# Attention and gated feed-forward on one core: output stages by a table of places, bias masks on PE for two batches, last keys on GpSimd

## The chip, the cores and the metric

The kernel runs on one core of a Trainium2 chip. The metric is the device time of one execution in microseconds (us). PE is the matrix engine (TensorE), ACT is ScalarE, DVE is VectorE, POOL is GpSimd, SP is SyncE, which only issues transfers here. PSUM is the memory that PE writes its results to; it has 8 banks of 512 fp32 columns, and one matmul writes at most one bank.

## The reference

Eight batches of 576 tokens, 8 heads of 64. Heads 0 to 3 look back over 32 tokens, heads 4 to 7 over 32 tokens at a distance of 4. The result, 4608 tokens of 512 features, goes through a gated feed-forward layer.

```python
batch, n_heads, seq, head_dim = (8, 8, 576, 64)
scores = scale * np.matmul(q, k.transpose(0, 1, 3, 2))
mask_plain = (rel >= 0) & (rel < window)
mask_dil = (rel >= 0) & (rel < window * dilation) & (rel % dilation == 0)
scores = np.where(masks[None, :, :, :], scores, -1000000000.0)
scores = scores - np.max(scores, axis=-1, keepdims=True)
attn = np.exp(scores)
attn = attn / (np.sum(attn, axis=-1, keepdims=True) + 1e-09)
out = np.matmul(attn, v)
...
n_tokens, d_model, d_ff = (4608, 512, 1536)
g = x @ w_gate
gelu = 0.5 * g * (1.0 + erf(g * inv_sqrt2))
val = x @ w_val
return (gelu * val @ w_out).astype(np.float32)
```

## The kernel before

All matmuls are fp16 with fp32 sums. The order of every engine is the order in which the program is written; no scheduler changes it.

**Attention** goes by pairs of heads: n = 0 to 31, four to a batch (n // 4), the first two of a batch plain, the last two dilated. A pair takes three steps. *Scores* (`emit_s`, L310): PE multiplies queries and keys into four PSUM banks (L329 plain, L359 dilated; the last keys of the dilated pairs come from a small copy `kTr`, made by `last_keys` on DVE, L240), and ACT takes the exponential into a tile P (L339 and L340, or L361). *Mask*: either DVE multiplies P by 0 and 1 (L369, `emit_mask`, put into the order later by `mask_next`), or, with `pe_mask`, PE first writes a bias of 0 and -60000 into the four banks by four matmuls with the identity (L322, L345), on which the scores are added, and no mask is needed; before the change the pairs 0 to 3, 6 and 7 do that. *Values* (`emit_pv`, L432): PE multiplies P by the values (the numerator) and by ones (the denominators) into three banks, V to V + 2; then DVE makes the reciprocal by two transposes (`norm_r`: L450, L452, L454) and writes the product to `xT` (`norm_x`: L465 plain, L468 dilated). Until `norm_x` has read them, the three banks aren't free for the next values.

**Feed-forward** goes by nine chunks of 512 tokens (c = 0 to 8). The first layer (`ffn1`, L480) takes 12 blocks `nb`; each writes a gate bank and a value bank, ACT applies Gelu to the gate (L504) and DVE multiplies into `u_all` (L505). Two pairs of banks alternate. `ffn1_two` (L492) does the first two blocks together, a quarter of the features at a time, so that the last quarter of `xT` may come late. The second layer (`ffn2`, L511) takes four blocks of 128 tokens, twelve matmuls `fc` each into one bank, which ACT evicts (`store`, L522), and SP sends out.

**How they are woven.** `mm0` is 0 or 4: the first layer works in the banks mm0 to mm0 + 3, the scores in the other four. In the output stages of chunks 1 to 5 the scores of the next pairs and the values of the last ones (`values_b`) are put between the matmuls of `ffn2`: scores after a block, right behind its eviction, and values inside the next block, at its `fc` 6, 4 and 2; every block but the first writes the bank mm0, the first one V = mm0 + 1. The first scores of a stage stand at the end of the first layer (L661). Where four pairs of values are done in a stage (c = 1 and 2), the fourth comes after the last block, `mm0` changes sides (`late = "x"`), and the next chunk begins with `ffn1_two`; after c = 3, 4 and 5 it stays (`late = "bank"`) and the two pairs of banks change their order.

```python
            ffn2(c, 1, mm0, {6: [pv]})
            store(c, 1, mm0, "act")
            s_next()
            ffn2(c, 2, mm0, {4: [pv]})
            store(c, 2, mm0, "act")
            s_next()
```

**Loads.** SP loads q, k and v of batch c + 2 in chunk c and issues the DMA transposes of the queries and keys (`qTp`, `qTd`); POOL casts to fp16 (L177, L190) and issues the loads of the dilated heads (`qd`, `rd`) and of the weights. In chunk 0 the transposes of batch 1 are done on PE (`t_plain`, `t_dil`, `t_rest`), between first-layer blocks 8 to 11.

Of the kernel before, what the change touches and what calls it, by code (L numbers as in the profile page):

```python
# [38 lines left out]
def kernel(  # L39
# [10 lines left out]
    nc = tc.nc  # L50
# [4 lines left out]
    NHP = H // 2  # L55
    HK = H // 2
# [157 lines left out]
    def load_batch_plain(b):  # L214
# [2 lines left out]
        v_plain(b, sv, nc.sync)  # L217
        return st, sv

    def load_batch_rest(b):  # L220
        st, sv = tiles["plain", b]
        qd, rd = load_qk_dil(b)
        qp = cast_qk_plain(b, st)
        load_v_dil(b)
        v_cast(b, sv)
        new_qt(b)
        qtp_, qtd_, _ = tiles["qT", b]
        dst = qtd_.rearrange("p t h m i -> p (t h m) i")
        nc.sync.dma_start_transpose(out=dst[:, :, 0:P], in_=qd.rearrange("p t h r d -> p (t h r d)"))
        nc.sync.dma_start_transpose(out=dst[:, :, P:NCL], in_=rd.rearrange("p t h r d -> p (t h r d)"))  # L230
        dst = qtp_.rearrange("p t h c -> p (t h) c")
        for kb in range(5):
            n = min(P, S - kb * P)
            nc.sync.dma_start_transpose(
                out=dst[:, :, kb * P : kb * P + n], in_=qp[0:n, kb].rearrange("p t h d -> p (t h d)")
            )

    def last_keys(b, h0, h1):
        _, qtd_, ktr = tiles["qT", b]
        nc.vector.tensor_copy(ktr[:, h0:h1], qtd_[:, 1, h0:h1, :, NCL - 64 : NCL])  # L240


    def is_plain(n):
# [66 lines left out]
    def emit_s(n, b0, pe_mask=False):  # L310

        b, hp = n // NHP, n % 2
        qtp_, qtd_, ktr = tiles["qT", b]
        st = not pe_mask
        mm = nc.tensor.matmul
        if n % NHP == 0 and n >= NHP:
            last_keys(b, 0, HK)
        if is_plain(n):
            if pe_mask:
                for i in range(4):  # L320
                    src = bias_p[:, 0:PB] if i % 2 == 0 else bias_p[:, PB:PH]
                    mm(ps[:, b0 + i, 0 : src.shape[1]], ident, src, start=True, stop=False, skip_group_check=True)  # L322
            for j in (0, 1, 2, 3, 4):
                for hl in range(2):
                    kt = qtp_[64 * hl : 64 * hl + 64, 1, hp, :]
                    qt = qtp_[64 * hl : 64 * hl + 64, 0, hp, :]
                    bank, c0 = b0 + 2 * hl + j // 3, (0, PW, 2 * PW, 0, P)[j]
                    k0, q0, w = (j * P, j * P, P if j == 3 else PW) if j < 4 else (S - P, S - PT, PT)
                    mm(  # L329
                        ps[:, bank, c0 : c0 + w],  # L330
                        kt[:, k0 : k0 + P],
                        qt[:, q0 : q0 + w],
                        start=st,
                        stop=True,
                        skip_group_check=True,
                    )
            pt = prb.tile([P, 2, PH], F16, tag="P", name=f"P{n}")
            sb = ps[:, b0 : b0 + 4, :].rearrange("p (h t) c -> p t h c", t=2)
            nc.scalar.activation(pt[:, :, 0:PB], sb[:, 0, :, 0:PB], AF.Exp, bias=0.0, scale=scale)  # L339
            nc.scalar.activation(pt[:, :, PB:PH], sb[:, 1, :, 0 : P + PT], AF.Exp, bias=0.0, scale=scale)  # L340
            reps, mask, w = 2, mask_p, PH
        else:
            if pe_mask:
                for i in range(4):
                    mm(ps[:, b0 + i, 0:DW], ident, bias_d, start=True, stop=False, skip_group_check=True)  # L345
            for hl in range(2):
                h = 2 * hp + hl
                for m in range(3):
                    for s in range(2):
                        half = slice(64 * s, 64 * s + 64)  # L350
                        bank = ps[:, b0 + 2 * s + hl, 0:DW]
                        if m < 2:
                            o = bank[:, m * NCL : m * NCL + P]
                            lhs, rhs = qtd_[half, 1, h, m, 0:P], qtd_[half, 0, h, m, 0:P]
                        else:
                            o = bank.rearrange("p (m i) -> p m i", m=2)[:, :, P:NCL]
                            lhs = ktr[half, h].rearrange("p m i -> p (m i)")
                            rhs = qtd_[half, 0, h, :, P:NCL]
                        mm(o, lhs, rhs, start=st, stop=True, skip_group_check=True)  # L359
            pt = prb.tile([P, 4, DW], F16, tag="P", name=f"P{n}")  # L360
            nc.scalar.activation(pt, ps[:, b0 : b0 + 4, 0:DW], AF.Exp, bias=0.0, scale=scale)  # L361
            reps, mask, w = 4, mask_d, DW
        tiles["P", n] = pt
        if pe_mask:
            return None

        def emit_mask():
            mb = bass.AP(tensor=mask.tensor, offset=mask.offset, ap=[mask.ap[0], [0, reps], [1, w]])
            nc.vector.tensor_tensor(pt, pt, mb, ALU.mult)  # L369

        return emit_mask
# [252 lines left out]
    scores = {0: range(4, 8), 1: range(8, 12), 2: range(12, 17), 3: range(17, 22), 4: range(22, 27), 5: range(27, 32)}  # L624
    values_b = {1: range(8, 12), 2: range(12, 16), 3: range(17, 20), 4: range(22, 24), 5: range(27, 28)}
    values_a = {3: {4: 16}, 4: {3: 20, 6: 21}, 5: {2: 24, 4: 25, 6: 26}, 6: {1: 28, 3: 29, 5: 30, 7: 31}}
    late = None
    for c in range(NCH):
        if 1 <= c and c + 2 < B:
# [2 lines left out]
        pv_at = values_a.get(c, {})  # L632
        s_list = list(scores.get(c, ()))
        pairs = (mm0, mm0 + 2)
        SB = 4 - mm0

        masks = []
        pend = None
        for nb in range(NNB):
            if nb == 0 and c < 2:  # L640
                ffn1_two(c, (4, 6) if c == 0 else (6, 0))
            elif nb == 0 and late == "x":
                ffn1_two(c, pairs)
            elif nb > 1 or c > 2 and late != "x":
                ffn1(c, nb, pairs[(nb + (c < 2 or late == "bank")) % 2])
            if pend is not None:
                norm_x(pend, SB)
                pend = None
            if nb in pv_at:
                pend = pv_at[nb]  # L650
                emit_pv(pend, SB, wide=True)
                norm_r(pend, SB, wide=True)
            if c == 0 and nb in (8, 9):
                t_plain(1, q61, nb - 8, 4 + 2 * (nb - 8), ("act", "dve"))
            if c == 0 and nb in (10, 11):
                rr = rd1.rearrange("p t h r d -> p t (h r d)")
                hp = nb - 10
                t_dil(1, hp, qd1, 4096 + 512 * hp, 5120 + 512 * hp, ("dve", "dve"))
                t_rest(1, hp, (rr[:, 0], rr[:, 1]), 6144 + P * hp)
            if nb == NNB - 1 and c > 0 and s_list:  # L660
                masks.append(emit_s(s_list.pop(0), SB))  # L661

        def s_next():
            if s_list:
                n = s_list.pop(0)
                masks.append(emit_s(n, SB, pe_mask=n in (6, 7)))

        def mask_next():
            mask = masks.pop(0) if masks else None
            if mask is not None:  # L670
                mask()

        def norm(n, b0):
            norm_r(n, b0)
            norm_x(n, b0)
# [8 lines left out]
        if c == 0:  # L684
# [9 lines left out]
            store(c, 3, 1, "act")  # L694
            num(6, 2)
            num(7, 4)
        elif c in values_b:
            todo = list(values_b[c])

            def pv(last=False):  # L700
                if todo and (len(todo) > 1 or last or len(values_b[c]) < 4):
                    n = todo.pop(0)
                    emit_pv(n, V)
                    if not last:
                        mask_next()
                    norm(n, V)

            mask_next()
            ffn2(c, 0, V)
            store(c, 0, V, "act")  # L710
            s_next()
            ffn2(c, 1, mm0, {6: [pv]})
            store(c, 1, mm0, "act")
            s_next()
            ffn2(c, 2, mm0, {4: [pv]})
            store(c, 2, mm0, "act")
            s_next()
            ffn2(c, 3, mm0, {2: [pv]})
            store(c, 3, mm0, "act")
            s_next()  # L720

            late = "bank"
            if todo:
                pv(last=True)
                mm0 = 4 - mm0
                late = "x"
            while masks:
                mask_next()
        else:
            late = None  # L730
            for tb in range(4):
                ffn2(c, tb, mm0 + tb)
                store(c, tb, mm0 + tb, "act" if tb < 3 else "dve")
# [1 line left out]
_INS = ['q', 'k', 'v', 'moe_w_gate', 'moe_w_val', 'moe_w_out']  # L735
_OUTS = [((4608, 512), 'float32')]
# [25 lines left out]
```

## Time and profile before

| | |
|---|---|
| median of 7 runs | 365.35 us (364.33 to 366.11) |
| profiled execution | 364.81 us; its span, first to last instruction, 362.9 us |
| granted clock of PE | 0.995 of full speed |
| busy: PE, DVE, ACT, POOL | 340.8, 193.7, 144.3, 75.9 us |
| chain that ended last | PE 72%, DMA 12%, DVE 9%, ACT 3%, POOL 2% |

The span begins with loads (until about 52 us, when the last output weights have landed), then chunk follows chunk. An output stage of chunks 1 to 5 begins at 88.24, 129.16, 169.07, 208.54 and 247.30 us. Of the profile's lists, a group is read as: line, engine, operation, tile written <- tiles read, shapes, count; the bracket of a timeline's line holds the idle time before it and what ended it. Matmul ends are modelled, so the lengths below go from start to start.

### The profile page before, as it was taken

How to read it: one execution, taken by the hardware profiler on the slowest of the kernel's cores; microseconds unless marked ns; L12 is line 12 of the kernel's file. 1: busy time of each engine (PE TensorE's matmuls, PEld its weight loads, DVE VectorE, ACT ScalarE, POOL GpSimd, SP SyncE). 2: the span in 40 equal slices, each digit the busy share in tenths (PEclk: the TensorE clock that was granted, in tenths of full speed). 3: DMA queues.
4: the chain of work that ended last, by engine and by line, in shares of the span. 5: the costliest groups of instructions: out<-in, count | busy, mean ns of one | idle time of the engine just before them, and what ended most of it. 6: DMA issues, size and time to landing. Idle time of an engine off the chain costs nothing.

```text
span 362.9 us, 6010 instructions
## 1 busy us (share of the span) xinstructions
PE 340.8 (94%) x2368; PEld 162.1 (45%) x2368; DVE 193.7 (53%) x292; ACT 144.3 (40%) x212; POOL 75.9 (21%) x104
## 2 busy tenths in 40 slices
PE   6889899999889999899989999999999999999995
PEld 2544444444444444444444444444444444444442
DVE  1584456643785348763766656783479413303320
ACT  2633345335333353525453355325542223312321
POOL 2580524530630620052004400150000000000000
PEclk9989999999999999999999999999999999999999
DMA  8999999999999991798149932795100030011002
GB/s 203 233 188 226 190 169 183 201 145 252 177 154 273 175 163 60 185 172 115 60 129 186 156 63 96 167 150 80 60 29 2 0 116 2 1 58 60 0 29 87
DMA packets 107291, 45.30 MB, mean 125 GB/s; under 512 B 83040, under 2 KB 102496, under 8 KB 107264
## 3 DMA queue, kind: packets, MB, share of 16 engines
q1 hardware_dynamic: 84272, 31.21, 39.8%
q0 software_dynamic: 21456, 12.01, 27.0%
q10 hardware_dynamic: 1536, 1.70, 2.1%
q8 instruction: 18, 0.29, 0.3%
q14 instruction: 9, 0.07, 0.1%
HBM read 40.13 MB, written 9.44 MB: 137 GB/s over the span
## 4 chain that ended last, share of the span: by engine, by line
PE 72%; DMA 12%; DVE 9%; ACT 3%; POOL 2%; issue 1%; ACTq 0%; SPq 0%; DVEq 0%; POOLq 0%
PE ps L480 42%; PE ps L511 22%; PE ps L432 4%; DMA xT<-in_k_dram 3%; DMA st<-in_k_dram 3%; DMA wv<-in_moe_w_val_dram 3%; DMA wo<-in_moe_w_out_dram 2%; DVE xT L468 2%; DVE rb L454 2%; DVE dt L450 2%; PE ps L492 2%; DVE P L369 1%; ACT osb L522 1%; DMA sv<-in_v_dram 1%; DVE u_all L505 1%; ACT P L361 1%
## 5 line engine op out<-in xcount | busy, mean ns | idle before, releaser
L505 DVE SCALAR_TENSOR_TENSOR u_all<-g,ps 128x512 f16<-128x512 f16 x108 | 73.6, 687 | 86.3 <-PE ps L480 76.8
L504 ACT ACTIVATE g<-ps 128x512 f16<-128x512 f32 x108 | 63.6, 597 | 123.8 <-PE ps L480 114.3
L511 PE MATMUL ps<-wo,u_all 128*128 128x512 f16 x432 | 101.0, 379 | 4.7 <-ACT osb L522 3.0
L480 PE MATMUL ps<-xT,wg 128*128 128x512 f16 x400 | 102.8, 379 | 1.3 <-DVE xT L468 1.1
L480 PE MATMUL ps<-xT,wv 128*128 128x512 f16 x400 | 102.6, 379 | 0.0
L511 PEld LDWEIGHTS <-u_all 128*128 128x128 f16 x432 | 39.8, 98 | 48.8 <-issue 4.9
L480 PEld LDWEIGHTS <-wv 128*128 128x128 f16 x400 | 39.2, 98 | 47.2
L480 PEld LDWEIGHTS <-wg 128*128 128x128 f16 x400 | 37.9, 98 | 46.4 <-issue 2.8
L522 ACT ACTIVATE osb<-ps 128x512 f32<-128x512 f32 x33 | 19.7, 597 | 66.2 <-PE ps L511 66.1
L190 POOL CAST qp<-st 128x2048 f16<-128x2048 f32 x6 | 11.4, 1896 | 109.9 <-DMA sv<-in_v_dram 74.9
L450 DVE STREAM_TRANSPOSE dt<-ps 128x576 f32<-128x576 f32 x32 | 24.9, 778 | 5.1 <-PE ps L432 4.8
L454 DVE STREAM_TRANSPOSE rb<-rc 128x576 f32<-128x576 f32 x32 | 24.9, 778 | 1.1
L369 DVE TENSOR_TENSOR P<-P,mask_p 128x1344 f16<-128x1344 f16 x14 | 13.3, 954 | 14.6 <-ACT P L340 14.6
L361 ACT ACTIVATE P<-ps 128x1152 f16<-128x1152 f32 x16 | 18.0, 1127 | 7.3 <-PE ps L359 7.3
L369 DVE TENSOR_TENSOR P<-P,mask_d 128x1152 f16<-128x1152 f16 x12 | 9.8, 820 | 15.7 <-ACT P L361 15.7
L468 DVE TENSOR_TENSOR xT<-ps,rb 128x576 f16<-128x576 f32 x16 | 17.9, 1127 | 0.4
L524 DVE TENSOR_SCALAR osb<-ps 128x512 f32<-128x512 f32 x3 | 2.1, 692 | 28.8 <-PE ps L511 28.8
L339 ACT ACTIVATE P<-ps 128x960 f16<-128x960 f32 x16 | 15.5, 968 | 1.5 <-PE ps L329 1.4
L432 PE MATMUL ps<-P,ones 128*64 128x96 f16 (+5 forms) x216 | 14.7, 248 | 1.1 <-ACT P L361 0.7
L492 PE MATMUL ps<-xT,wg 128*128 128x512 f16 x32 | 12.2, 380 | 0.9 <-DVE xT L468 0.9
L492 PE MATMUL ps<-xT,wv 128*128 128x512 f16 x32 | 12.1, 379 | 0.5 <-DMA wv<-in_moe_w_val_dram 0.5
L465 DVE TENSOR_TENSOR xT<-ps,rb 128x576 f16<-128x576 f32 x16 | 11.9, 750 | 0.8 <-PE ps L432 0.5
(74 smaller groups left out, 232.2 us busy)
## 6 DMA issues: line engine op xcount, KB each, us to landing
out_dram<-osb SPq DMA_DIRECT2D x36, 256.0 KB, 2.0
sv<-in_v_dram SPq DMA_DIRECT2D x40, 128.0 KB, 3.5
st<-in_q_dram SPq DMA_DIRECT2D x24, 128.0 KB, 3.1
st<-in_k_dram SPq DMA_DIRECT2D x24, 128.0 KB, 3.3
qd<-in_q_dram POOLq DMA_DIRECT2D x7, 256.0 KB, 5.4
qd<-in_k_dram POOLq DMA_DIRECT2D x7, 256.0 KB, 7.1
vd<-in_v_dram POOLq DMA_DIRECT2D x7, 256.0 KB, 7.3
wg<-in_moe_w_gate_dram POOLq DMA_DIRECT2D x3, 512.0 KB, 7.3
```

The lines of the kernel that those rows point to most:

```text
L361: nc.scalar.activation(pt, ps[:, b0 : b0 + 4, 0:DW], AF.Exp, bias=0.0, scale=scale)
L369: nc.vector.tensor_tensor(pt, pt, mb, ALU.mult)
L432: nc.tensor.matmul(o, lhs, rhs, start=st, stop=True, skip_group_check=True)
L450: nc.vector.transpose(dst, den)
L454: nc.vector.transpose(rb.rearrange("p (b c) -> p b c", c=32), bass.AP(tensor=rc.tensor, offset=rc.offset, ap=[rc.ap[0], [1, 18], [0, 32]]),)
L468: nc.vector.tensor_tensor(dst.rearrange("p (i m s) -> p i m s", m=2, s=2), num, rb.rearrange("p (s m i) -> p i m s", s=2, m=2), ALU.mult,)
L480: nc.tensor.matmul(ps[:, b0 + gi, :], w[:, kc, ns], xT[kc][:, tok], start=(kc == 0), stop=(kc == NKC - 1))
L492: nc.tensor.matmul(ps[:, pairs[nb] + gi, :], w[:, kc, ns], xT[kc][:, tok], start=(kc == 0), stop=(kc == NKC - 1),)
L504: nc.scalar.activation(g, ps[:, b0, :], AF.Gelu)
L505: nc.vector.scalar_tensor_tensor(u_all[:, nb, :], g, USCALE, ps[:, b0 + 1, :], ALU.mult, ALU.mult)
L511: nc.tensor.matmul(ps[:, bank, :], u_all[:, fc, tb * P : (tb + 1) * P], wo_t[fc // 4][:, fc % 4, :], start=(fc == 0), stop=(fc == NNB - 1),)
L522: nc.scalar.activation(osb, ps[:, bank, :], AF.Copy, bias=0.0, scale=1.0 / USCALE)
```

## The change

The output stages of chunks 1 to 5 are now laid out by a table. An entry such as `2.6v` means: in block 2, before matmul 6, the values of the next pair; `1.12s` means: after block 1 and its eviction, the scores of the next pair. Within a stage scores and values alternate so that some stand at block boundaries too.

Beside that: pairs 8 to 15 (batches 2 and 3) get their mask as a bias on PE. `last_keys` of batches 2 to 7 is a copy by GpSimd at the end of the batch's load. The first output block of a stage writes a bank of the first-layer pair that was used last but one (`first`). The bank side `mm0` now changes after chunk 3 too (more than two pairs of values), and chunk 4 begins with `ffn1_two`. In chunk 0 the PE transposes of batch 1 change order: dilated pair 0 after block 8, plain ones after 9 and 10, dilated pair 1 after 11.

```diff
+    def last_keys(b, h0, h1, eng=nc.vector):
+        _, qtd_, ktr = tiles["qT", b]
+        eng.tensor_copy(ktr[:, h0:h1], qtd_[:, 1, h0:h1, :, NCL - 64 : NCL])
...
+        last_keys(b, 0, HK, nc.gpsimd)
...
-        if n % NHP == 0 and n >= NHP:
+        if n == NHP:
             last_keys(b, 0, HK)
...
+    biased = (6, 7, 8, 9, 10, 11, 12, 13, 14, 15)
+    four = "1.5s 1.9v 1.12s 2.6v 2.12s 3.3v 3.12s 3.12v"
+    three = "1.4s 1.12v 2.3s 2.12v 3.2s 3.12s 3.12v"
+    two = "1.4s 1.12v 2.3s 2.12v 3.2s 3.12s"
+    one = "1.4s 1.12v 2.3s 2.12s 3.6s"
+    places = {1: four, 2: four, 3: three, 4: two, 5: one}
...
-            if c == 0 and nb in (8, 9):
-                t_plain(1, q61, nb - 8, 4 + 2 * (nb - 8), ("act", "dve"))
-            if c == 0 and nb in (10, 11):
+            if c == 0 and nb in (9, 10):
+                t_plain(1, q61, nb - 9, 4 + 2 * (nb - 9), ("act", "dve"))
+            if c == 0 and nb in (8, 11):
...
-                masks.append(emit_s(n, SB, pe_mask=n in (6, 7)))
+                masks.append(emit_s(n, SB, pe_mask=n in biased))
...
+            first = pairs[(NNB - 2 + swap) % 2] + (pairs[(NNB - 2 + swap) % 2] == mm0)
+
+            def pv(last):
+                n = todo.pop(0)
+                emit_pv(n, V)
+                if not last:
+                    mask_next()
+                norm(n, V)
...
+                bank = mm0 + tb if not lone else first if tb == 0 else mm0
+                ffn2(c, tb, bank, hooks)
+                store(c, tb, bank, "dve" if c > 5 and tb == 3 else "act")
+                for fc, kind in at:
+                    if fc == NNB:
+                        do(kind, True)
+            if lone:
+                late = "bank"
+                if len(values_b[c]) > 2:
+                    mm0 = 4 - mm0
+                    late = "x"
```

## The prediction

> **What bounds the kernel now.** I read the page first, then the windows of the five output stages that the change rewrites, then PE's waits, then PE's timeline inside them.
>
> ```profile
> span 362.9 us, 6010 instructions
> ...
> PE 340.8 (94%) x2368; PEld 162.1 (45%) x2368; DVE 193.7 (53%) x292; ACT 144.3 (40%) x212; POOL 75.9 (21%) x104
> ```
>
> PE is the bound, the others are half idle. So only two things count: work added to PE, and holes in PE.
>
> ```profile
> 88.24:107.62 19.38, 15.85 (x173) 8.27 (x173) 14.03 (x18) 9.34 (x12) 9.48 (x11) 1.00 1.24 171
> 129.16:146.72 17.56, 16.06 (x184) 8.29 (x183) 12.28 (x19) 9.54 (x14) 1.03 (x2) 1.00 0.55 112
> 169.07:186.20 17.13, 15.41 (x163) 7.76 (x163) 12.50 (x18) 9.09 (x13) 0.00 (x0) 1.00 0.26 64
> 208.54:224.19 15.65, 14.55 (x146) 7.21 (x145) 9.96 (x14) 7.94 (x11) 0.00 (x0) 1.00 0.28 70
> 247.30:262.09 14.79, 13.71 (x125) 6.63 (x125) 7.00 (x10) 7.93 (x11) 0.00 (x0) 1.00 0.17 59
> ```
>
> Each row is one output stage, c = 1 to 5, from the end of its first-layer matmuls to the first matmul of the next chunk; the second figure is its length, the third PE's busy time. PE idles 3.53, 1.50, 1.72, 1.10 and 1.08 us: 8.9 us in all. The clock is 1.00, so nothing is to be had there.
>
> ```profile
> PE ps L511 <- ACT osb L522: 3.0, 10, 0.3
> PE ps L432 <- DVE xT L468: 2.1, 3, 1.1
> PE ps L511 <- DVE u_all L505: 1.4, 3, 0.5
> PE ps L432 <- DVE xT L465: 1.3, 1, 1.3
> ```
>
> Ten waits for the evicted bank, three for the last `u_all`, the rest for the bank of the values before.
>
> ```profile
> 89.25 2.75 PE L511 MATMUL ps<-wo,u_all 128*128 128x512 f16 x12 [0.45 <-DVE u_all L505]
> 91.93 0.47 PE L329 MATMUL ps<-qTp 64*128 64x160 f16 x10
> 92.33 1.47 PE L511 MATMUL ps<-wo,u_all 128*128 128x512 f16 x6
> ...
> 96.60 1.02 PE L511 MATMUL ps<-wo,u_all 128*128 128x512 f16 x4 [0.31 <-ACT osb L522]
> 98.88 0.45 PE L432 MATMUL ps<-P,vp 128*64 128x160 f16 x8 [1.25 <-DVE xT L465]
> ...
> 106.96 0.30 PE L432 MATMUL ps<-P,vd 128*64 128x128 f16 x4 [1.08 <-DVE xT L468]
> ```
>
> This is stage 1: the first output block waits for `u_all`; scores of 0.40 stand between two blocks, shorter than the eviction of the bank, so PE waits 0.31 more; and the values of a head pair wait until DVE has turned the values before into `xT` and so emptied their banks, 1.25 and 1.08.
>
> ```profile
> 212.34 0.60 ACT L522 ACTIVATE osb<-ps 128x512 f32<-128x512 f32 x1 [1.42 <-PE ps L511]
> 212.83 1.12 ACT L361 ACTIVATE P<-ps 128x1152 f16<-128x1152 f32 x1
> ...
> 220.98 0.96 ACT L339 ACTIVATE P<-ps 128x960 f16<-128x960 f32 x1
> 221.83 0.50 ACT L340 ACTIVATE P<-ps 128x384 f16<-128x384 f32 x1
> ```
>
> On ACT an exponential starts 0.49 after an eviction's start, and a plain one ends 1.35 after its own start (220.98 to 221.83 + 0.50).
>
> **Prices, from starts in PE's timeline (us).** An L511 matmul 0.216 (twelve 2.59). Plain scores 0.50 (91.93 to 92.33 is 0.40, and 0.10 to switch in); dilated 0.47. Values: plain 0.81 (0.09 in, 174.03 to 174.75), dilated 0.75 (214.00 to 214.66). A bank is writable again 0.85 after its block's last slot (slot end 95.75, eviction 95.95 to 96.55, matmul 96.60). Values to values, when nothing else is in DVE's way: plain 3.56 (174.03 to xT's end at 177.54, and 0.05), dilated 3.89 (214.00 to 217.89).
>
> **Bias on PE, n = 8 to 15.** Four matmuls each. Dilated: four L345 take 0.49 (59.99 to 60.48 on the chain of waits, with the switch that scores pay anyway). Plain: no row in a warm stage; below, 0.49 for fewer columns (1152 against 1344); above, 0.67, the two prologue groups of L322 (10.51 to 11.18, 11.58 to 12.25) with 0.10 of switch in it. I take 0.57, L345 scaled by columns and equally 0.67 less the switch. Sum 4 x (0.57 + 0.49) = 4.24 on PE. By the Trainium skill (TensorE: Matmul & The Clock Gate, Back-to-back issue gap) sustained 512-column matmuls come every 131 ns, which would make the bias an estimated 2.6 and the time 361.7 instead of the forecast below. In this trace they come every 216 ns, over twelve at 89.25 as anywhere, and that decides. DVE loses eight L369 masks (0.86 and 0.76; two were stretched to 2.24 and 1.50).
>
> **The stages, walked from 0 at the end of the first layer.** A comma is the next step of PE; "free" is when a wait lets go.
>
> *c = 1.* Biased scores 8 to 1.07, block 0 to 3.66: it goes to bank 2, freed a block earlier, so the 0.45 for `u_all` goes; the bias that now stands ahead covers the rest. Five matmuls to 4.74, biased scores 9 to 5.81, four to 6.67, values 8 (start 6.76) to 7.49, three to 8.14. Bank free 8.99; biased scores 10 last to 9.10: no wait. Six to 10.40, values 9 start 10.49 (free 6.76 + 3.56 = 10.32) to 11.22, six to 12.52, scores 11 to 13.48 (free 13.37), three to 14.13, values 10 start 14.22 (free 14.05) to 14.88, nine to 16.82. Values 11 wait for values 10: 14.22 + 3.89 = 18.11, to 18.77. Before 19.38: **-0.61**. The 1.2 wait at the end stays.
>
> *c = 2.* The same walk to 16.80 (banks 5 and 4 are free, no `u_all` wait before either), then unbiased scores 16 to 17.30; values 15 at 18.09, to 18.75. Before 17.56: **+1.19**. It had no `u_all` wait and small eviction waits, so 2.12 of bias buys 0.93.
>
> *c = 3.* Scores 17 to 0.50, sixteen to 3.95, scores 18 to 4.42, eight to 6.15, values 17 to 6.96, free 7.00, three to 7.65, scores 19 to 8.12, nine to 10.06, values 18 to 10.81, free 10.91, two to 11.34, scores 20 to 11.84, ten to 14.00, scores 21 to 14.50, values 19 (start 14.59) to 15.25. The banks now swap here, so the next chunk begins in the banks of scores 21: eviction from 14.19, their exponentials from 14.68 to 16.05, and the second matmul goes at 16.10 instead of 15.47, 0.63 late. The last quarter waits for values 19 (18.48), to 19.34; 0.20 for `g` as after c = 1 and 2 now; masks 20 and 21 (2 x 0.86) stand before `u_all` on DVE: 0.49. The third pair ends at 21.75; before at 17.13 + 24 x 0.216 = 22.31: **-0.56**.
>
> *c = 4.* Scores 22 to 0.47 and no `u_all` wait (the pairs' order changes with the swap), sixteen to 3.92, scores to 4.39, eight to 6.12, values 22 to 6.87, free 6.97, three to 7.62, scores to 8.12, nine to 10.06, values 23 (free 10.10, start 10.15) to 10.81, free 10.91, two, scores to 11.84, ten, scores 26 to 14.47. Before 15.65: **-1.18**.
>
> *c = 5.* Scores 27 to 0.47, sixteen to 3.92, scores to 4.42, eight, values 27 to 6.90, free 7.00, three, scores to 8.15, nine to 10.09, scores 30 to 10.56, free 10.94, six, scores 31 to 12.71, six to 14.01. Before 14.79: **-0.78**.
>
> **What costs nothing.** Last keys on GpSimd: no row for this copy; 0.49 (128x256, L178) to 1.05 (128x1024, L177), I take 0.72 (128x512, L250). It waits for both transposes, and behind it stand the next batch's `qd` loads: issued at 102.04 before, at most 104.48 + 0.72 = 105.2 now, landing near 113.4 instead of 110.24. SP transposes them from 119.09: 5 us of cover; keys are wanted later still. Without cover it would be the 3.2. DVE's 0.29 each was no wait of PE. Chunk 0: dilated transposes now come first and wait for `rd` (landed 42.68) instead of the 1.08 for `qp`; PE is some 0.25 later, but it waits for `wo` (landed 52.54) in either case, arriving at 52.18 before. Below nothing this can't go: that landing hangs on loads and POOL alone.
>
> **Sum.** -0.61 + 1.19 - 0.56 - 1.18 - 0.78 = -1.94. Span 362.9 to 361.0; the profiled execution took 364.81, 1.9 of it outside the span, so 362.87. The median of the runs is 365.35, and I state the forecast against it: 363.4.
>
> **Rivals.** *Slower: the hooks come too early.* In c = 1 and 2 values 9, 10, 13 and 14 start 0.17 after their bank is free. If DVE needs e longer than the rows, PE waits at two hooks, all matmuls of the output block queued behind, and again at the last values: 2 (e - 0.17) + e = 3e - 0.34 a stage. From e = 0.44 the gain is gone; at 0.8 it is 6 x 0.8 - 0.68 = 4.12 lost, 367.5. For it: the trace has 93.73 to 98.88, 5.15 instead of 3.56. Against: that was the 2.24 mask, beside a POOL cast, and it is gone. The Trainium skill (SBUF — State Buffer, Who interferes with whom) lets GpSimd's reads block only a VectorE operation with two SBUF inputs or a two-port mode; by it L465 stays clear and e is nothing. Chance 0.14.
>
> *No change.* The hand-over after c = 3 costs more than walked, because `u_all` is behind the two masks: if both are paid in full, 1.72 instead of 0.49, and the plain bias costs 0.67 (4 x 0.10 more), 1.94 - 1.23 - 0.40 = 0.31 is left: 365.0. For it: the chunk now starts in the banks emptied last; against: `u_all` waits for `g` anyhow. Chance 0.12.
>
> *More.* That hand-over is free (0.63 + 0.20 + 0.49 less), as it is before the change, where the next chunk starts in other banks: 362.1. Against: ACT's order is written, and store 3 and scores 21 stand right ahead. Chance 0.12. That the built program doesn't do it is excluded: its order has the bias matmuls before n = 8 to 15 and the new places.
>
> **Numbers.** My sum 0.62. Range 361.8 to 365.2: down to the free hand-over with 0.3 of spread, up to e = 0.43. The measurement tells about 0.2%, 0.73 us. Faster 0.62 + 0.12 = 0.74, same 0.12, slower 0.14.
>
> **What would show it.** Right: the five stages become 18.8, 18.8, 15.7 (to the first matmul; 0.9 of it is given back in the next 3.5 us), 14.5 and 14.0 long; "PE L511 <- DVE u_all" vanishes; "PE L511 <- ACT osb" falls from 3.0 to about 0.8; eight masks fewer on DVE. Wrong: waits of the values' matmuls for `xT` above 0.2 at 2.6v and 3.3v, or new waits for `qTd` or `kTr`.

## The result and the profile after

The changed kernel takes 364.19 us (median of 25 runs, 362.49 to 366.01) beside 365.57 for the kernel before (64 runs): a ratio of 0.9961, 95% interval 0.9951 to 0.9972, so 1.0 to 1.8 us faster. The forecast was 1.95 us faster, 363.4 us. The profiled execution took 364.58 us at a granted clock of 0.984 (before: 364.81 at 0.995). In the changed kernel the lines stand a little lower than before: L511 is now L512, L432 is L433, the masks' L369 is L370, L522 is L523.

The head of the page after:

```profile
span 362.5 us, 6061 instructions
...
PE 347.2 (96%) x2400; PEld 165.8 (46%) x2400; DVE 185.7 (51%) x278; ACT 146.1 (40%) x212; POOL 78.3 (22%) x110
```

PE is busy for 6.4 us more and the span is 0.4 shorter: the change bought out holes and paid for it in matmuls. Not all of the 6.4 is added work. Some 3.8 lie in stages 1 and 2, where the bias was added (17.66 and 18.07 below, 15.85 and 16.06 before); 2.3 lie in the first 53 us, where about the same matmuls ran at a lower granted clock in this execution (0.90 up to 53.78 us, before 0.97 up to 52.58). The windows of the five stages, as before from the last first-layer matmul's slot to the first matmul of the next chunk, and as fourth row the first layer that follows stage 3 (start:end, length, PE busy):

```profile
90.08:108.84 18.76, 17.66 (x189) 9.15 (x187) 8.80 (x13) 9.69 (x12) 7.23 (x10) 1.00 1.11 160
130.40:149.19 18.79, 18.07 (x200) 9.58 (x198) 8.82 (x13) 9.73 (x13) 3.09 (x5) 1.00 0.66 118
171.52:187.27 15.75, 15.23 (x163) 7.70 (x163) 8.97 (x13) 9.53 (x13) 0.00 (x0) 1.00 0.33 78
187.27:210.07 22.80, 22.75 (x128) 10.19 (x127) 16.33 (x25) 8.70 (x15) 8.86 (x12) 1.00 0.95 168
210.07:224.57 14.50, 14.45 (x145) 7.03 (x145) 9.37 (x13) 8.28 (x11) 0.00 (x0) 1.00 0.38 85
247.66:261.70 14.04, 13.70 (x126) 6.57 (x126) 6.83 (x10) 9.04 (x11) 0.00 (x0) 1.00 0.16 59
```

Walked were 18.77, 18.75, 15.7, 14.47 and 14.01. PE now idles 1.10, 0.72, 0.52, 0.05 and 0.34 in them, 2.7 us against 8.9. PE's waits from 90 us to the end of stage 5 (releaser: us in total, times, longest):

```profile
PE ps L433 <- DVE xT L469: 1.8, 2, 1.1
PE ps L493 <- DVE xT L469: 0.9, 2, 0.5
PE ps L493 <- ACT P L340: 0.5, 1, 0.5
PE ps L512 <- ACT osb L523: 0.3, 1, 0.3
```

The wait for the last `u_all` is gone, that for the evicted bank is down from 3.0 in ten to 0.3 in one. That one stands in stage 5; what else is left stands at the ends of stages 1 and 2, in the first layers behind them, and at the hand-over after stage 3. PE's timeline of stage 1 shows the beginning and the end:

```profile
90.08 0.73 PE L323 MATMUL ps<-bias_p,ident 128*128 128x480 f16 x4
...
91.14 3.84 PE L512 MATMUL ps<-wo,u_all 128*128 128x512 f16 x17
...
108.18 0.30 PE L433 MATMUL ps<-P,vd 128*64 128x128 f16 x4 [1.10 <-DVE xT L469]
```

Seventeen output matmuls run without a hole (from 91.14) where twelve had waited 0.45 before; the last values still wait 1.10 for DVE.

### The profile page after: what moved, and what is told of

It reads as the page before. It is cut to its first block, busy times and chain, and to the rows that moved or that the text cites. A ratio compares the mean times of both kernels' runs of the same rounds, so it can differ in the third digit from the quotient of the medians.

```text
span 362.5 us, 6061 instructions
## 1 busy us (share of the span) xinstructions
PE 347.2 (96%) x2400; PEld 165.8 (46%) x2400; DVE 185.7 (51%) x278; ACT 146.1 (40%) x212; POOL 78.3 (22%) x110
## 4 chain that ended last, share of the span: by engine, by line
PE 78%; DMA 13%; DVE 4%; POOL 2%; ACT 1%; issue 0%; SPq 0%; ACTq 0%; POOLq 0%; DVEq 0%
PE ps L481 41%; PE ps L512 25%; PE ps L433 5%; DMA xT<-in_k_dram 3%; DMA st<-in_k_dram 3%; DMA wv<-in_moe_w_val_dram 3%; PE ps L493 3%; DMA wo<-in_moe_w_out_dram 2%; DVE xT L469 1%; PE ps L360 1%; DMA sv<-in_v_dram 1%; PE ps L330 1%; DVE dt L451 1%; DVE rb L455 1%; DMA out_dram<-osb 1%; PE ps L346 1%
## 5 line engine op out<-in xcount | busy, mean ns | idle before, releaser
L512 PE MATMUL ps<-wo,u_all 128*128 128x512 f16 x432 | 101.1, 380 | 0.6 <-ACT osb L523 0.3
L512 PEld LDWEIGHTS <-u_all 128*128 128x128 f16 x432 | 39.2, 98 | 44.9 <-issue 1.0
L481 PEld LDWEIGHTS <-wv 128*128 128x128 f16 x392 | 38.3, 98 | 46.4 <-issue 0.2
L523 ACT ACTIVATE osb<-ps 128x512 f32<-128x512 f32 x33 | 19.7, 598 | 48.4 <-PE ps L512 48.4
L433 PE MATMUL ps<-P,ones 128*64 128x96 f16 (+5 forms) x216 | 15.1, 254 | 2.0 <-ACT P L362 1.0
L370 DVE TENSOR_TENSOR P<-P,mask_p 128x1344 f16<-128x1344 f16 x10 | 9.1, 914 | 6.8 <-ACT P L341 6.8
L370 DVE TENSOR_TENSOR P<-P,mask_d 128x1152 f16<-128x1152 f16 x8 | 6.1, 757 | 11.1 <-ACT P L362 11.1
```

What stands on the lines that cost most here:

```text
L433: nc.tensor.matmul(o, lhs, rhs, start=st, stop=True, skip_group_check=True)
L481: nc.tensor.matmul(ps[:, b0 + gi, :], w[:, kc, ns], xT[kc][:, tok], start=(kc == 0), stop=(kc == NKC - 1))
L512: nc.tensor.matmul(ps[:, bank, :], u_all[:, fc, tb * P : (tb + 1) * P], wo_t[fc // 4][:, fc % 4, :], start=(fc == 0), stop=(fc == NNB - 1),)
L523: nc.scalar.activation(osb, ps[:, bank, :], AF.Copy, bias=0.0, scale=1.0 / USCALE)
```

## Experiments

Stage lengths below are by the same windows: from the end of the first layer's last slot.

**Was stage 1 of before really 19.38 long?** The kernel before twice more, nothing edited.

> The kernel before, unchanged: a second look at its start and its stage 1. Theory A (after the trace of the old stages behind the new chunk 0 showed stage 1 at 18.2 us and chunk 1 starting at 89.9): the first trace of before was lucky in its start (88.3) and unlucky in stage 1 (19.3), because masks and GpSimd's casts met; here chunk 1's output stage starts at 89 to 90.5 us and stage 1 is 18.0 to 19.4 us, the later the start, the shorter or longer as the masks meet the casts; stages 2 to 5 stay 17.5, 17.0, 15.6, 14.7. Rival: stage 1 is 19.3 and the start 88.3 again, and the new order of chunk 0 makes the difference.

> The kernel before, unchanged, a third look: as for the second. Theory A: the start of stage 1 and its length differ from look to look by 0.5 us or more, stages 2 to 5 by less than 0.05. Rival: all are as in the first trace.

Measured: 365.02 and 364.61 us. The output stage of chunk 1 began at 89.26 and 89.39 us. Stages 2 to 5 agree with the first trace within 0.02 us. Stage 1 was 18.55 and 18.05 long, against 19.38 in the trace that the prediction used; a fourth trace with the same stage 1 (the old table with the new chunk 0, below) has 18.31. The rows that differ, all engines, first the trace of the prediction:

```profile
93.55 1.90 POOL L190 CAST qp<-st 128x2048 f16<-128x2048 f32 x1 [13.28 <-DMA sv<-in_v_dram]
...
93.91 2.24 DVE L369 TENSOR_TENSOR P<-P,mask_p 128x1344 f16<-128x1344 f16 x1 [2.19 <-ACT P L340]
```

and the second of the new ones:

```profile
95.07 0.86 DVE L369 TENSOR_TENSOR P<-P,mask_p 128x1344 f16<-128x1344 f16 x1 [2.18 <-ACT P L340]
...
95.68 2.00 POOL L190 CAST qp<-st 128x2048 f16<-128x2048 f32 x1 [14.56 <-DMA st<-in_k_dram]
```

The mask of pair 9 takes 2.24 when GpSimd's cast began 0.36 ahead of it, and 0.86 when it began 0.61 ahead of the cast. The other two traces lie between; the first of the new ones, then the one with the new chunk 0:

```profile
93.75 1.89 POOL L190 CAST qp<-st 128x2048 f16<-128x2048 f32 x1 [14.16 <-DMA st<-in_k_dram]
94.93 1.42 DVE L369 TENSOR_TENSOR P<-P,mask_p 128x1344 f16<-128x1344 f16 x1 [2.19 <-ACT P L340]
```
```profile
94.07 1.89 POOL L190 CAST qp<-st 128x2048 f16<-128x2048 f32 x1 [13.68 <-DMA sv<-in_v_dram]
95.49 1.18 DVE L369 TENSOR_TENSOR P<-P,mask_p 128x1344 f16<-128x1344 f16 x1 [2.18 <-ACT P L340]
```

In the three traces where the cast came first, the mask ends 0.70 to 0.71 after the cast, and the stage goes with the mask: 19.38, 18.55, 18.31 and 18.05 long for masks of 2.24, 1.42, 1.18 and 0.86. When that cast comes depends on when its data land (the bracket), so stage 1 differs from run to run. The Trainium skill says that a VectorE operation with two SBUF inputs contends with a GpSimd instruction that reads SBUF, and that the order of issue decides which of them blocks (SBUF — State Buffer, Who interferes with whom); these rows agree. Over the four traces stage 1 of before is 18.57 long on average; after the change, which has no mask there, six traces give 18.76 to 18.78. So the stage did not become 0.6 shorter, but some 0.2 longer than those four were on average.

**Does the bias pay?** The changed kernel with the bias taken off pairs 8 to 15, and with it for batch 2 alone; then the kernel before with the bias alone.

```diff
-    biased = (6, 7, 8, 9, 10, 11, 12, 13, 14, 15)
+    biased = (6, 7)                      # e2_no_bias
+    biased = (6, 7, 8, 9, 10, 11)        # e3_bias_batch2
```
```diff
-                masks.append(emit_s(s_list.pop(0), SB))
+                n = s_list.pop(0)
+                masks.append(emit_s(n, SB, pe_mask=n in range(6, 16)))
...
-                masks.append(emit_s(n, SB, pe_mask=n in (6, 7)))
+                masks.append(emit_s(n, SB, pe_mask=n in range(6, 16)))   # e6_before_bias
```

> The changed kernel with the masks of pairs 8 to 15 on DVE again. Theory A (walk with the prediction's prices): the 4.24 us of bias go from PE, the masks come into DVE's chain. Stage 2, where GpSimd casts nothing, falls from 18.8 to 17.9 us. In stage 1 masks 9 and 10 fall into GpSimd's casts and are stretched: 17.9 without stretching, 19.4 with two stretches of 0.7 to 1.4 us. In all 0.9 us faster to 0.6 slower than the changed kernel. Rival: the bias pays in both stages, because DVE's chain is what values wait for; then both stages grow, to 19.5 or more, and the time rises by 1.4 us or more.

> The changed kernel with the bias for batch 2 alone (pairs 8 to 11); batch 3 has masks on DVE. Theory A: stage 1 stays 18.8 us, stage 2 falls to 17.9, the time falls by 0.9 us against the changed kernel, to 0.9937 of the kernel before. Rival (the bias pays in both): stage 2 grows to 19.5, the time rises by 0.7 us.

> The kernel before with the bias masks of pairs 8 to 15 on PE and nothing else. Theory A (the prediction's prices walked in the old order): stage 1 falls from 19.3 to 18.5 us, since the bias fills the waits for the evicted bank and for u_all, stage 2 grows from 17.5 to 18.5; in all 0.1 us, the same time as before within 0.1%; the table of places is then worth nothing in these two stages. Rival: the bias needs the new places to fill the waits; then both stages grow by 1 to 2 us and the time is 2 to 3 us longer.

Measured: 363.34 us without the new biases (7 runs; ratio to before 0.9951, 0.9934 to 0.9969), 363.52 with batch 2's alone (6; 0.9949, 0.993 to 0.9968), and 366.48 for the kernel before with all of them (12; 1.0026, 1.001 to 1.0043). Stages 1 and 2 of the kernel without:

```profile
89.68:108.33 18.65, 15.79 (x174) 8.20 (x173) 12.82 (x17) 9.47 (x12) 8.99 (x11) 1.00 1.14 149
129.88:147.92 18.04, 16.12 (x183) 8.41 (x183) 11.78 (x17) 9.64 (x14) 3.09 (x5) 1.00 0.83 131
```

PE has 1.9 us less work in each stage (third figure, 15.79 against 17.66), but the stages are only 0.11 and 0.75 shorter: both end when DVE has done the norms of three pairs, one after the other, and the bias mostly fills time that PE would spend waiting. In stage 1 of this trace the masks of pairs 9 and 10 were stretched as well, to 1.23 and 1.51 from 0.86 and 0.76; so without such stretching the bias may be dearer there. In the old order the bias makes stage 2 18.56 long instead of 17.56, and leaves stage 1 at 18.57. Where it was put, then, the bias costs about 0.9 us in the new order by the stage lengths, and 0.9 in the old one by the times (366.48 against 365.59 for the kernel before beside it). In the new order the times alone don't show it: 363.34 is 0.85 below 364.19, but as ratios to the kernel before it is 0.9951 against 0.9961, with intervals that overlap.

**What else was in the change.** The old order of chunk 0's transposes in the changed kernel (e1) and the new order in the kernel before (e5); the last keys on DVE again (e7); the first output block in V, the bank of the values, as before (e8, one run).

```diff
-            if c == 0 and nb in (9, 10):
-                t_plain(1, q61, nb - 9, 4 + 2 * (nb - 9), ("act", "dve"))
-            if c == 0 and nb in (8, 11):
+            if c == 0 and nb in (8, 9):
+                t_plain(1, q61, nb - 8, 4 + 2 * (nb - 8), ("act", "dve"))
+            if c == 0 and nb in (10, 11):          # e1_old_chunk0; e5 is the reverse, in the kernel before
...
-        last_keys(b, 0, HK, nc.gpsimd)
...
-        if n == NHP:
+        if n % NHP == 0 and n >= NHP:              # e7_dve_keys
...
-                bank = mm0 + tb if not lone else first if tb == 0 else mm0
+                bank = mm0 + tb if not lone else V if tb == 0 else mm0      # e8_block0_in_V
```

> The changed kernel with the order of batch 1's PE transposes in chunk 0 put back (plain pairs after blocks 8 and 9, dilated ones after 10 and 11). Theory A, the prediction's: chunk 0 ends on the landing of the last output weights in either order, so the time is that of the changed kernel, 0.9961 of the kernel before, within 0.1%, and the stages of chunks 1 to 5 stay 18.8, 18.8, 15.8, 14.5, 14.0 us. Theory B: the missing part of the forecast gain (1.94 forecast, some 1.4 measured) was lost in chunk 0, where PE now waits for the dilated rows; then the time falls by 0.5 us or more, to 0.9947 or less.

> The kernel before with the changed order of batch 1's transposes in chunk 0 and nothing else; its trace is also a second look at the old output stages behind another start. Theory A (the new order is hidden by the wait for the last output weights): 1.000 of the kernel before within 0.1%. Theory B (the new order costs what is missing of the forecast): 0.4 to 0.9 us slower, 1.001 to 1.0025. On the stages, theory A: they are fixed and stay 19.3, 17.5, 17.0, 15.6, 14.7 us, so that the whole of the missing part lies ahead of chunk 1. Rival: stage 1 of the one trace of before was unlucky, with two masks stretched by GpSimd's casts; then it is shorter here, 18.0 to 18.8 us, and the gain of the change was never 2.2.

> The changed kernel with the last keys copied by DVE again, at the first scores of each batch. Theory A: DVE's 0.29 us copies wait for nobody, and the five stages keep 18.8, 18.8, 15.6, 14.4 and 13.9 us within 0.1. Outside the span the changed kernel spends 2.08 us (median of 25) against 1.9 to 1.95 before and in the kernels that are before with one edit; if GpSimd's copies are the reason, it is 1.95 here and the time falls by 0.15, else it stays 2.08. Rival: the copies sit in DVE's chains of stages 1 and 2 and lengthen each by 0.3 us.

> The changed kernel with the first output block of a stage in bank V again. Theory A: in stage 1 the bias covers the wait for u_all, in 3 and 4 the two banks are the same, so only stage 5 grows, by 0.5 us (13.9 to 14.4). Rival: the freed bank matters in every stage with the other order of pairs, 0.4 to 0.5 us in stage 1 too.

*Chunk 0*: 363.77 us with the old order in the changed kernel (12 runs; 0.9965, 0.9952 to 0.9977), the same as the change itself; 365.25 with the new order in the kernel before (12; 0.9989, 0.9971 to 1.0006). Neither swap moves the time by more than the intervals, about 0.6 us each way. The begin of stage 1 scatters by more than that: from 88.2 to 89.8 us in five traces with the old order (mean 89.3) and from 89.3 to 90.6 in nine with the new one (mean 89.9). So a cost of some tenths stays open. The reason that was given for a cost of nothing, that PE waits for the last output weights in either order, holds in the traces of before and after, but in only five of the fourteen in all; in these two PE comes when the weights are already there.

*Keys*: 364.16 us on DVE again (12 runs; 0.9957, 0.9939 to 0.9974): no difference. The two groups, of the changed kernel and of this one:

```profile
L222 POOL COPY kTr<-qTd x6: 614/615/617, 78.8 to 245.4; 128x512 f16<-128x512 f16 x6
```
```profile
L222 DVE COPY kTr<-qTd x8: 280/290/434, 18.3 to 251.3; 128x512 f16<-128x512 f16 x8
```

GpSimd takes 0.615 us for what DVE does in 0.29; the prediction had taken 0.72. Nothing on PE waits for either. One small thing does go with it. The time that a run takes beyond its span is 1.94 us at the median for the kernel before, 2.08 for the changed one, 2.07 to 2.15 for every other variant of several runs with keys on GpSimd, and 1.96 for this one: some 0.13 us that no row of the span shows.

*First block*: 365.28 us in one run; its stages 1 to 4 are as in the changed kernel, stage 5 is 0.53 longer. PE's timeline there:

```profile
248.76 2.10 PE L512 MATMUL ps<-wo,u_all 128*128 128x512 f16 x9 [0.48 <-DVE u_all L506]
```

In the changed kernel that block begins without a wait:

```profile
248.15 2.76 PE L512 MATMUL ps<-wo,u_all 128*128 128x512 f16 x12
```

So the freed bank does take the `u_all` wait away, and that was worth 0.5 us, in stage 5. The edit says little of the others: by the kernel's text `first` is V itself in stages 2, 3 and 4, and another bank only in 1 and 5. In stage 1 V costs nothing, with the four bias matmuls standing ahead of the block.

**The ends that are left.** Stage 3's last scores moved ahead of its last values (e4); then, beside that, the values of stages 1 and 2 placed earlier, with pairs 8 and 12 off the bias (v1).

```diff
-    three = "1.4s 1.12v 2.3s 2.12v 3.2s 3.12s 3.12v"
+    three = "1.4s 1.12v 2.3s 2.12v 3.2s 3.8s 3.10v"        # e4_scores21_early, and v1
...
-    biased = (6, 7, 8, 9, 10, 11, 12, 13, 14, 15)
+    biased = (6, 7, 9, 10, 11, 13, 14, 15)                 # v1_values_early
-    four = "1.5s 1.9v 1.12s 2.6v 2.12s 3.3v 3.12s 3.12v"
+    four = "1.4v 1.5s 1.12v 2.1s 2.9v 2.12s 3.8v"
+    five = "1.4v 1.5s 1.12v 2.1s 2.9v 2.12s 3.6s 3.8v"
-    places = {1: four, 2: four, 3: three, 4: two, 5: one}
+    places = {1: four, 2: five, 3: three, 4: two, 5: one}
...
-                        pv(after and tb == 3)
+                        pv(after and tb == 3 or c == 2 and len(todo) == 1)
```

> The changed kernel with the end of stage 3 moved forward: scores 21 before matmul 8 of the last block, values 19 before its matmul 10. Theory A: the wait of the next chunk's first matmuls for the exponential of scores 21 goes (0.5 and 0.1 us in the changed kernel's trace); what is late next is xT of values 19, whose place moves by 0.43: 0.4 us less in all. Rival: the exponential was all that was late, and the masks' delay goes with it: 1.1 us less.

> A version from these readings: in stages 1 and 2 the values stand earlier (before matmul 4 of block 1, after block 1, before matmul 9 of block 2, before matmul 8 of block 3), the first pair of each batch is masked on DVE and the other three by the bias, and stage 3 ends as in the kernel with scores 21 early. Theory A: stages 1 and 2 are then bound by PE's own work and not by the chain of DVE: 17.0 and 17.5 us instead of 18.8 each, and the wait of 0.6 us in the following first layer goes too; with 0.4 in stage 3, 4.6 us less than the changed kernel, 0.983 of the kernel before. Rival: the waits only move, since DVE's chain of four values is 14 us however it is placed; then 1 us less.

e4: 363.74 us (8 runs; 0.9963, 0.9945 to 0.9982). The times can't tell it from the change; its trace can: stage 3 is 0.35 shorter and the first layer behind it 0.09, and PE no longer waits there for the exponentials. v1: **359.95 us** (4 runs, 359.65 to 360.61; 0.9849, 0.9827 to 0.987), 4.2 us faster than the changed kernel, and faster than both. Its stages 1 and 2:

```profile
89.77:106.87 17.10, 17.10 (x185) 8.88 (x185) 10.43 (x15) 7.99 (x10) 6.00 (x8) 1.00 1.13 156
127.80:145.39 17.59, 17.59 (x196) 9.12 (x196) 10.45 (x15) 9.34 (x12) 3.52 (x7) 1.00 0.95 137
```

PE is busy for the whole of both, 1.66 and 1.20 shorter than in the changed kernel. Of that, 0.56 and 0.48 are work that PE no longer has (17.66 to 17.10, 18.07 to 17.59), as pairs 8 and 12 have no bias; 1.10 and 0.72 are the holes that were left. Since the last values come four matmuls before the end, the first layers behind them lose their waits too, 0.63 each.

**Is the bias only a cost, then?** v1 without its biases; each mask goes on DVE right ahead of its own values, as v1's order needs.

```diff
-    biased = (6, 7, 9, 10, 11, 13, 14, 15)
+    biased = (6, 7)
...
                 n = todo.pop(0)
-                emit_pv(n, V)
-                if not last:
+                if not last or c < 3:
                     mask_next()
+                emit_pv(n, V)
```

> The order of v1 (values early, 359.95 us; stages 1 and 2 are 17.0 and 17.5 long), with the biases of pairs 9, 10, 11, 13, 14 and 15 taken off PE again; each pair's mask goes on DVE right ahead of its values, since in that order the values follow the scores of the same pair. Theory A (a bias matmul is PE work and nothing else, as taking it out of the changed kernel suggested): each of the two stages loses 0.57 + 2 x 0.49 = 1.55 of PE work, 15.5 and 15.95 long, 356.9 us. Theory B (in this order the bias buys something: a mask would stand in DVE's chain between the norms of one pair and the values of the next): norm 8 ends at 97.45 in v1, mask 9 adds 0.86, values 9 can start at 98.3 where PE could be there at 96.9; norm 9 to 101.9, mask 10 0.76, values 10 at 102.7; norm 10 to 106.5, mask 11, values 11 at 107.3, to 108.05, and four matmuls 0.86: 108.9, a stage of 19.0 instead of 17.0, the next about 19.5, with PE's waits for P at L370 at three hooks a stage, 1.4, 1.2 and 1.0: about 364.0 us. More than that if a mask meets a cast of GpSimd.

Measured: 362.71 us (6 runs, 361.98 to 363.83; 0.9918, 0.9892 to 0.9943), 2.8 slower than v1. Theory A, by which a bias is PE work and nothing else, falls: it asked for 356.9. Theory B has the mechanism: values wait for their masks (L433 for P at L370) 2.22 and 0.50 in stage 1, 1.31 and 0.92 in stage 2, two hooks a stage where it had named three; its 364.0 was 1.3 high. The windows of the profiled execution (363.69 us, near the upper end of the runs), stages 1 and 2, and a piece of stage 1; the figure after the engines is the granted clock:

```profile
89.38:109.63 20.25, 17.12 (x173) 8.99 (x173) 13.43 (x18) 7.87 (x10) 8.94 (x12) 0.92 1.10 159
130.56:149.35 18.79, 16.25 (x184) 8.50 (x183) 12.55 (x18) 9.22 (x12) 3.08 (x5) 1.00 0.54 101
98.77:101.17 2.40, 2.40 (x33) 1.67 (x33) 1.00 (x2) 0.00 (x0) 1.18 (x2) 0.50 0.98 90
```

and what came before that piece (a cast of GpSimd follows at 98.44):

```profile
96.48 0.76 POOL L204 DMA_DIRECT2D vd<-in_v_dram  x1
...
96.98 1.73 DVE L370 TENSOR_TENSOR P<-P,mask_p 128x1344 f16<-128x1344 f16 x1
97.23 1.24 POOL L209 DMA_DIRECT2D vr<-in_v_dram  x2
...
98.44 1.16 POOL L177 CAST vp<-sv 128x1024 f16<-128x1024 f32 x1
98.77 0.72 PE L433 MATMUL ps<-P,vp 128*64 128x160 f16 x8 [2.22 <-DVE P L370]
```

Mask 9 takes 1.73 instead of 0.86, PE waits 2.22 for it, and then runs at half its clock for more than 3 us: the same view gives 0.50 up to 101.60 and 1.00 again from 102.00. In these traces the bias saves 3.15 and 1.20 us of the two stages; the first holds the stretched mask and the slow clock behind it, so the 2.8 between the medians is the better figure for its worth in this order.

## Why the prediction was right, and where its sizes were off

Faster, inside the range, by the forecast's own mechanism: holes of PE closed in stages 3, 4 and 5, paid for with bias in stage 2. But the gain is 1.38 us (1.0 to 1.8), not 1.95. The terms, all by the same windows; stage 1 of before once as in the trace used, once as the mean of four traces:

| term | predicted | against that trace | against the mean |
|---|---|---|---|
| stage 1 | -0.61 | -0.62 | +0.19 |
| stage 2 | +1.19 | +1.23 | +1.23 |
| stage 3 and hand-over | -0.56 | -0.92 | -0.92 |
| stage 4 | -1.18 | -1.15 | -1.15 |
| stage 5 | -0.78 | -0.75 | -0.75 |
| outside the span | 0 | +0.14 | +0.14 |
| sum | -1.94 | -2.07 | -1.26 |

The table leaves out the time ahead of stage 1, which the prediction put at no difference. In the two profiled executions it is 1.84 us longer after the change (90.08 against 88.24), and -2.07 + 1.84 is the -0.23 by which they differ (364.58 against 364.81). Over the other traces that begin scatters by as much, as said above, so it isn't booked to the change.

*The walk* was right: four of the five lengths came within 0.04 us and stage 3's within 0.05. That the waits of stages 3 to 5 are gone is read from the traces; beside the first block's bank in stage 5 and the end of stage 3, no experiment puts the old places of these stages back. Bias groups of 0.57 and 0.49 were priced exactly; the chain that ended last has 0.57 for the four at L323 and 0.49 for the four at L346. Output matmuls came every 216 ns here at a granted clock of 1.00: seventeen from 91.14 take 3.68 us. The 131 ns of the Trainium skill (TensorE: Matmul & The Clock Gate, Back-to-back issue gap) and the 361.7 estimated from it did not come.

*Stage 1, mis-sized.* The 18.77 was right; the 19.38 that it was taken from was not typical. The trace held the 2.24 mask, and the text named it, used it against the first rival, and still subtracted from a stage that contained it. With the mean the term is +0.19, 0.8 us worse. That the hand-over after stage 3 came out 0.36 better hid nearly half of this, which is luck. The 0.45 of `u_all` was put down to the freed bank and the bias together; with block 0 in V again stage 1 is as long, so the bias alone covers it.

*Hand-over after stage 3, mis-sized.* It gave 0.63 + 0.20 + 0.49. From the timelines of PE and DVE:

```profile
187.27 0.38 PE L493 MATMUL ps<-xT,wg 128*128 128x512 f16 x1 [0.49 <-ACT P L340]
...
187.66 0.38 PE L493 MATMUL ps<-xT,wv 128*128 128x512 f16 x1
...
189.80 1.62 DVE L370 TENSOR_TENSOR P<-P,mask_p 128x1344 f16<-128x1344 f16 x2
...
191.09 1.02 PE L481 MATMUL ps<-xT,wg 128*128 128x512 f16 x4
191.34 1.28 DVE L506 SCALAR_TENSOR_TENSOR u_all<-g,ps 128x512 f16<-128x512 f16 x2
192.07 1.02 PE L481 MATMUL ps<-xT,wv 128*128 128x512 f16 x4
```

The second matmul goes 16.14 after the stage's begin (walked: 16.10), the wait for `g` is 0.20 (190.67 + 0.22 to 191.09); that is 0.49 + 0.17 + 0.20. The two masks do stand where they were put, but the whole first layer is only 0.46 longer than before (22.80 against 22.34), so of their 0.49 about 0.1 reached PE: the value matmuls start at 192.07, four slots of 0.216 behind 191.09 would be 191.95. The rows show why. The walk let the masks begin at 18.48 after the stage's begin and gave them 2 x 0.86, to 20.20; in the trace they begin at 18.28 (189.80) and `u_all` starts at 19.82 (191.34), nearly 0.4 earlier.

*The rivals.* Slower, the hooks too early: refuted, as values 9 and 10 (starts 100.58 and 104.31) don't wait for `xT` at all. But it was close: `xT` of values 8 ends 3.65 after their start, where the price was taken from 3.51, so e was 0.14 there, just below the 0.17 that the places allow. No change, by a dearer hand-over: refuted, it was cheaper. More, by a free one: of its 1.32 us some 0.36 were free, and the other errors outweighed that. *What costs nothing* held for the keys, but for 0.13 us outside the span, and for chunk 0 within the 0.6 us of the intervals, though not for the reason given.

## What to carry to other kernels

Before a difference is taken between a walk and a trace, ask of each row in the trace whether it would be there again: a row stretched by a neighbour (2.24 against 0.86) belongs to the noise, not to the base. When an engine's holes end on a serial chain elsewhere (here the norms on DVE), start that chain earlier before giving the waiting engine more work; with the chain early, PE had no hole left in two stages, and the whole version gained 4.2 us, some 1.0 of it from bias matmuls that it drops. And the worth of moving work between engines (the bias) has no sign of its own: the bias of eight pairs cost 0.9 us under one order, and that of six of them saved 2.8 under another.

## What the runs showed of the hardware

A pause of 2.22 us on PE (up to 98.77) was followed by a granted clock of 0.50 until about 102.0, while pauses of 1.31 and 0.92 us in stage 2 of the same run left it at 1.00. The Trainium skill (TensorE: Matmul & The Clock Gate, What's actually happening) gives an idle window of about 3.4 us before the clock falls. Here less was enough.

A mask was also stretched ahead of any cast: to 1.73 us in the last experiment, where GpSimd only issued DMAs beside it until its cast at 98.44, 0.27 before the mask's end (the rows above). What stretched it was not tested.
